# A new order of the loads, of K's first transform products and of the whole plan in a fused SSM convolution and gated MLP

## The chip, the cores and the metric

The kernel runs on one core of a Trainium2 chip. The time is that of the device in microseconds for one launch, and the median over several executions is compared. The core has five engines that work side by side: PE (matmul), DVE (vector), ACT (activations), POOL (GpSimd) and SP, which here only issues transfers. Each engine takes its instructions in order. SP, ACT and POOL can issue transfers between the memory outside the core (DRAM) and the one inside (SBUF); the products of PE go to PSUM and are evicted from there by DVE or ACT.

## What is computed

A layer norm, a long convolution whose filter K is generated from a state space model, and a gated MLP, both on the normalized tokens, added to the input. There are 2048 tokens of 512 channels, 128 modes for each channel, and 1792 hidden columns; all tensors are bf16.

```python
xn = _layernorm(x)
# A: K = sum over modes n of C * exp(dt*A*l) * dt*B, l = 0 .. 2047, real part
P = jnp.exp(logdA[:, :, None] * l[None, None, :])
K = jnp.einsum("dn,dnl,dn->dl", Cc, P, dB).real
...
Yf = Uf * Kf[None, :, :, :]          # FFTs of 4096 of u = xn and of K
y = irfft2(Yf)[..., :L] + u * Dskip
# B:
h = _sigmoid(xn @ w_gate) * (xn @ w_up)
return x + y + h @ w_down
```

## The kernel before, in words

**The MLP** (`glu`). The tokens are worked in eight groups of 256. For each group PE multiplies the transposed tokens xnT with the up and the gate weights (tile W, 14 column blocks of 128 in chunks of four, L827; one product task is eight matmuls of 128x256), ACT takes the sigmoid, DVE multiplies, and PE multiplies with the down weights wd (L832). Group 0 and group 1 have their tokens transposed on PE (the "turn", L496, copied out as xnT by L358 on ACT or L359 on DVE); later groups by transfers. For group 0 the up products come first, then the gate ones. The last product of the group adds the input by a matmul with the identity (L837).

**The filter** (`params`, `hlevels`, `glevels`, `kgen`, `expand`). The parameters (six arrays, loaded in halves as raw00 to raw51: array, then block) become powers H and G by repeated complex multiplication on DVE (L645 to L648), in two blocks b of 256 channels with two halves c each. `kgen` multiplies them on PE (L732) and gets K, which is written to DRAM (kt_scr) and read back by `expand` in 19 shifted pieces to the tile kf.

**The convolution** is a transform in two steps. `spectrum_x` and `spectrum_k` make the first step's products with a constant matrix s1p (L790 for the tokens, L810 for K, eight products for a block: four groups m of four kf columns, two halves j), evict them and write them to DRAM (z_scr, zk_scr). `freq` reads these back in another layout, eight units per block: px and pkf (L960) are the second step's products, XX is their pointwise product (L980 on DVE, or L981 on ACT and then DVE), pv (L969) goes back one step, and its eviction G is written to v_scr. `inverse` reads v_scr (as tiles H, G, kf) and makes the last step's products py (L1008), which DVE adds to the output (L1012). `store` writes the output.

**The plan.** Each piece of work is one of 919 tasks, numbered in the order in which the functions add them. A planner outside the kernel has chosen three tables by its own costs, sizes and dependencies; at run time only the tables count. `emit` goes through ORDER and calls the tasks one after the other, so ORDER sets the order on every engine and queue. OTHER lists the tasks that run on their alternative engine: evictions and norms change between ACT and DVE, transfers between the queues of SP and POOL. SIDE picks, for each PSUM buffer, one of four areas A to D. Semaphore waits come from the overlap of the tiles that tasks read and write, in program order. The arguments `after`, `mb`, `rank` and the helper `seq`, which adds an edge between two tasks, only tell the planner what it may not do or what a transfer costs.

**The loads** (`loads`). SP issues nearly all. x0 and x1 (128 KB each), x2 (256 KB), x4, x8, x12 (512 KB each) are tokens; w1 with its start column (0, 512, 1024 with 512 KB each; 1536 with 256 KB) are the up weights, w0 the gate weights; the raw pieces have 64 KB; wd0 (1 MB) and wd8 (768 KB) are the down weights. The order on SP before: x0, raw00, ldt, x2, x8, raw20, raw40, raw50, raw30, raw41, w1 0, x4, w1 512, w1 1024, w1 1536, w0 0, x12, w0 512, w0 1536, w0 1024, raw21, raw51, raw11, raw01, wd8, raw31, wd0.

Tasks that the prediction names: 767, 702, 780, 741 and 832 are issues of SP in the late stage (reads of zk_scr for units 0, 1 and 5 of the second block, and writes of v_scr for units 4 and 7 of the first); 804 and 830 write v_scr for units 2 and 4 of the second block; norms 2, 4, 6, 14, 15 are the layer norm of one row block of 128 tokens each.

Of the kernel before, what the change touches and what calls it, by code (L numbers as in the profile page):

```python
# [24 lines left out]
NT = 16  # L25
# [4 lines left out]
ND = 256  # L30
# [187 lines left out]
class _Kernel:  # L218
# [145 lines left out]
    def loads(self):  # L364
# [39 lines left out]
        n0 = len(self.ld)  # L404
# [3 lines left out]
        for q in range(2, 6):  # L408
            raw(q, 0, mb=0.09)
# [12 lines left out]
        self.seq([self.ld["x0"], self.ld["raw00"]] + list(self.ld.values())[n0:n0 + 2])  # L422
        for t in list(self.ld.values())[n0 + 2:]:
            self.seq([self.ld["x2"], t])
# [324 lines left out]
    def expand(self, b):  # L749

        kf, kt, rk = self.kf[:].rearrange("p (i d) -> p i d", d=ND), self.kt_scr[b], 82 + 70 * b
        rows = kt[:].rearrange("h g d -> (h g) d")
        kfb = self.own("kf")
# [4 lines left out]
        def rd(out, in_, n):  # L758
            self.kfl.append(self.dma(lambda: out, lambda: in_, 1.7 * n * ND * 2 / 1048576, self.dump, rk, 512, alt="POOL", more=0.12,
                                     **(dict(use=[kfb]) if self.kfl else dict(take=[kfb]))))  # L760

        for i in range(2):
            rd(kf[0:16, 8 * i:8 * i + 8, :], kt[0:8, i::2, :].rearrange("h g d -> g h d"), 128)
        for v, r0 in enumerate((256, 256, 512, 544, 544, 544, 576, 257)):
            rd(kf[16:32, v::8, :], rows[r0:r0 + 32].rearrange("(p i) d -> p i d", i=2), 32)
        for v, n, r0 in ((0, 3, 288), (3, 3, 608), (6, 2, 289)):
            for i in range(2):
                rd(kf[32:64, 8 * i + v:8 * i + v + n, :], rows[r0 + i:r0 + i + 63:2].unsqueeze(1).to_broadcast([32, n, ND]), 32 * n)
        for v, n, r0 in ((0, 5, 352), (5, 7, 353), (12, 4, 354)):
            rd(kf[64:128, v:v + n, :], rows[r0:r0 + 127:2].unsqueeze(1).to_broadcast([64, n, ND]), 64 * n)  # L770
# [4 lines left out]
        self.kfls[b], self.kfbs[b] = self.kfl + [self.kfd], kfb  # L775
# [22 lines left out]
    def spectrum_k(self, b):  # L798
# [4 lines left out]
        for m in range(NT // 4):  # L803
            for j in range(2):
# [7 lines left out]
                t = add("PE", 0.44, mm, self.kfls[b] + [self.ld["s1p"]], rk, take=[pz], use=[self.kfbs[b]])  # L812
# [293 lines left out]
```

## Time and profile before

| | us |
|---|---|
| three executions | 231.98, 232.03, 233.49 |
| median | 232.03 |
| profiled execution, its own time | 232.98 |
| its span, first to last instruction | 231.2 |

The mean granted clock of PE is 0.999. The profiled execution is 1.8 us longer than its span (launch and end around it), and it is 0.95 us above the median. In the rows below times are us from the start of the span. A timeline row shows the start, the time until the last of its instructions ended, engine, line, operation and tiles, how many instructions were joined (xN), and in brackets how long the engine had been idle before and what ended that.

### The profile page before, as it was taken

The numbers are of one execution on the slowest core, as the hardware profiler recorded it, in microseconds if no ns is written. First come the engines' busy times: TensorE is split into PE (matmuls) and PEld (weight loads), VectorE is DVE, ScalarE is ACT, GpSimd is POOL, SyncE is SP. The second block draws the span as 40 slices with busy tenths as digits, with TensorE's granted clock in tenths as the row PEclk, the third lists the DMA queues.
The fourth block names the chain that finished last, engine by engine and source line by source line (L and its number), as shares of the span: only waits on it lengthen the run. The fifth ranks groups of instructions, "written<-read, shape, count | busy, mean of one in ns | idle before, by whom it ended". The sixth has DMA issues, their size and how long they took to land.

```text
span 231.2 us, 5364 instructions
## 1 busy us (share of the span) xinstructions
PE 212.2 (92%) x2150; PEld 148.7 (64%) x2169; DVE 200.1 (87%) x301; ACT 173.6 (75%) x218; POOL 40.2 (17%) x66
## 2 busy tenths in 40 slices
PE   3679998999999999999999999999988968999993
PEld 0368886677578876687446888667744545676641
DVE  3799989999999999999998999857697899958492
ACT  3199999999999989997754895427796589893500
POOL 2110060000010000050404121146020514011300
PEclk9999999999999999999999999999999999999999
DMA  6999911112212425435759888469878899995866
GB/s 164 246 331 348 315 60 34 25 23 71 91 57 48 115 31 136 116 91 138 220 198 284 291 255 240 100 166 224 217 269 286 235 285 295 303 269 161 257 252 220
DMA packets 55643, 43.16 MB, mean 187 GB/s; under 512 B 20785, under 2 KB 48642, under 8 KB 55362
## 3 DMA queue, kind: packets, MB, share of 16 engines
q1 hardware_dynamic: 51890, 33.16, 50.0%
q0 software_dynamic: 3312, 9.45, 13.2%
q8 instruction: 17, 0.28, 0.5%
q10 hardware_dynamic: 416, 0.20, 0.3%
q14 instruction: 8, 0.07, 0.1%
HBM read 25.86 MB, written 15.37 MB: 178 GB/s over the span
## 4 chain that ended last, share of the span: by engine, by line
PE 50%; ACT 20%; DMA 13%; DVE 11%; issue 3%; SPq 1%; ACTq 0%; DVEq 0%
PE po L832 15%; PE pg L827 12%; PE pu L827 9%; PE pk L732 4%; DMA zk<-zk_scr 4%; DMA zk_scr<-G 3%; DMA H<-v_scr 3%; PE pzx L790 2%; ACT ub L884 2%; DVE tB L645 2%; DMA acc<-in_A_u_dram 2%; DVE G L646 2%; PE pkf L960 2%; PE py L1008 2%; DVE G L647 1%
## 5 line engine op out<-in xcount | busy, mean ns | idle before, releaser
L827 PEld LDWEIGHTS <-W 128*128 128x128 bf16 x896 | 86.8, 98 | 19.5 <-issue 3.9
L827 PE MATMUL pg<-xnT,W 128*128 128x256 bf16 x496 | 60.5, 273 | 0.9 <-ACT ub L884 0.2
L827 PE MATMUL pu<-xnT,W 128*128 128x256 bf16 x400 | 47.6, 273 | 1.5 <-DMA W<-in_B_w_up_dram 1.1
L832 PE MATMUL po<-wd,hT 128*128 128x512 bf16 x133 | 31.9, 379 | 1.1 <-ACT hTb L358 0.6
L980 DVE TENSOR_TENSOR XX<-pkf,x 128x1024 bf16<-128x1024 f32 x20 | 23.9, 1221 | 6.4 <-PE pkf L960 6.1
L832 PEld LDWEIGHTS <-hT 128*128 128x128 bf16 x140 | 13.5, 98 | 15.8 <-issue 1.2
L892 ACT ACTIVATE ub<-pu 128x1024 bf16<-128x1024 f32 x16 | 16.5, 1030 | 5.3 <-PE pu L827 5.2
L645 DVE TENSOR_TENSOR tB<-G,gm 128x256 bf16<-128x256 bf16 (+4 forms) x20 | 19.6, 980 | 0.9 <-ACT G L707 0.6
L646 DVE TENSOR_TENSOR G<-G,gm 128x256 bf16<-128x256 bf16 (+4 forms) x20 | 19.6, 979 | 0.1
L889 ACT ACTIVATE hT<-pg 128x1024 bf16<-128x1024 f32 (+1 forms) x16 | 14.9, 928 | 6.0 <-PE pg L827 6.0
L358 ACT ACTIVATE zs<-pzx 128x1024 bf16<-128x1024 f32 x16 | 16.3, 1038 | 1.9 <-PE pzx L790 1.3
L358 ACT ACTIVATE x<-px 128x1024 bf16<-128x1024 f32 x14 | 14.3, 1027 | 4.2 <-PE px L960 3.3
L981 ACT ACTIVATE XX<-pkf 128x1024 bf16<-128x1024 f32 x12 | 12.2, 1027 | 6.3 <-PE pkf L960 6.3
L960 PEld LDWEIGHTS <-w 64*64 64x64 bf16 x384 | 9.7, 105 | 10.3 <-issue 8.7
L457 DVE BATCH_NORM_STATS2 stats<-acc 128x6 f32<-128x512 bf16 x16 | 10.6, 681 | 5.2 <-DMA acc<-in_A_u_dram 5.2
L960 PE MATMUL pkf<-zk,w 64*64 64x256 bf16 x256 | 12.3, 276 | 3.0 <-DMA zk<-zk_scr 1.1
L350 POOL DMA_DIRECT2D kf<-kt_scr x14 | 8.0, 581 | 29.0 <-DMA kt_scr<-ks 29.0
L358 ACT ACTIVATE G<-pv 128x1024 bf16<-128x1024 f32 x12 | 12.4, 1041 | 0.5 <-PE pkf L960 0.5
L832 PE MATMUL po<-wd,hTb 128*128 128x512 bf16 x55 | 12.7, 379 | 0.0
L891 DVE TENSOR_TENSOR hT<-hT,ub 128x1024 bf16<-128x1024 bf16 (+1 forms) x15 | 9.4, 632 | 3.4 <-ACT ub L892 3.4
L647 DVE TENSOR_TENSOR G<-G,tB 128x128 bf16<-128x128 bf16 (+4 forms) x20 | 11.4, 571 | 0.5
L648 DVE TENSOR_TENSOR G<-G,tB 128x128 bf16<-128x128 bf16 (+4 forms) x20 | 11.3, 566 | 0.1
(144 smaller groups left out, 356.1 us busy)
## 6 DMA issues: line engine op xcount, KB each, us to landing
z_scr<-zs SPq DMA_DIRECT2D x12, 256.0 KB, 2.3
zk<-zk_scr SPq DMA_DIRECT2D x11, 256.0 KB, 5.1
v_scr<-G SPq DMA_DIRECT2D x11, 256.0 KB, 4.9
acc<-in_A_u_dram SPq DMA_DIRECT2D x3, 512.0 KB, 6.3
W<-in_B_w_up_dram SPq DMA_DIRECT2D x3, 512.0 KB, 7.2
W<-in_B_w_gate_dram SPq DMA_DIRECT2D x3, 512.0 KB, 8.4
zk_scr<-G SPq DMA_DIRECT2D x6, 256.0 KB, 2.7
out_dram<-acc SPq DMA_DIRECT2D x6, 256.0 KB, 2.3
```

The lines of the kernel that those rows point to most:

```text
L358: return self.p.add("ACT", 0.17 + n / 1190, lambda: nc.scalar.activation(out=dst(), in_=src(), func=ACT.Identity), after, rank, alt=("DVE" ...
L645: ops = [(2, lambda: tt(out=tv(), in0=l, in1=mb(1), op=ALU.mult), [], [tB], []), (2, lambda: tt(out=o, in0=l, in1=mb(0), op=ALU.mult), [], ...
L646: (2, lambda: tt(out=o, in0=l, in1=mb(0), op=ALU.mult), [], [], []),
L647: (1, lambda: tt(out=o[:, :, 0], in0=o[:, :, 0], in1=tv()[:, :, 1], op=ALU.add), [0, 1], [], [tB]),
L648: (1, lambda: tt(out=o[:, :, 1], in0=o[:, :, 1], in1=tv()[:, :, 0], op=ALU.subtract), [0, 1], [], [tB])]
L827: nc.tensor.matmul(p[:, lo + n, :], W[:, i, kt, k * 128:(k + 1) * 128], xT[:, kt, :], start=kt == 0, stop=kt == KT - 1)
L832: nc.tensor.matmul(po[:, jj, :], hT[:, k, jj * 128:(jj + 1) * 128], wd[:, k, :], start=k == 0, stop=k == FT - 1 and self.outs[i // GT].eng ...
L889: e1 = add("ACT", 0.17 + n * 256 / 1190, lambda hk=hk, n=n, pg=pg: nc.scalar.activation(out=hk(), in_=pg[:, 0:n, :], func=ACT.Sigmoid), mg ...
L892: e2 = add("ACT", 0.17 + n * 256 / 1190, lambda uk=uk, pk=pk: nc.scalar.activation(out=uk(), in_=pk(), func=ACT.Identity), mu + [e1], rk + ...
L960: nc.tensor.matmul(p[o:o + 64, par, h, :], self.w3[i:i + 64, w, 64 * g:64 * g + 64], z[i:i + 64, 2 * h + c, :], start=True, stop=True, til ...
L980: prod = lambda xo=xo, x1=x1, src=None: nc.vector.tensor_tensor(out=xo(), in0=src(), in1=x1[:, 0], op=ALU.mult)
L981: ek = add("ACT", 1.03, lambda xo=xo, flat=flat: nc.scalar.activation(out=xo(), in_=flat(), func=ACT.Identity), [mk, e] + ([] if o else se ...
```

## The change

It changes four things. The number of tasks and their numbering stay as they are.

1. The planner is told a larger size for the four transfers raw20 to raw50 (0.15 MB in place of 0.09).
2. Behind x0 and raw00 the next eight loads are fixed: ldt, x2, w1 0, raw20, raw30, raw40, raw50, w1 512; all others may come only behind w1 512. Before, only ldt and x2 were fixed.
3. In `expand` each read notes which groups m of K's first products use its columns, and a product in `spectrum_k` depends, for the planner, on the reads of its own group alone (and on the add of Dskip for group 0) in place of on all 19.
4. New tables ORDER, OTHER and SIDE.

```diff
         for q in range(2, 6):
-            raw(q, 0, mb=0.09)
+            raw(q, 0, mb=0.15)
...
-        self.seq([self.ld["x0"], self.ld["raw00"]] + list(self.ld.values())[n0:n0 + 2])
-        for t in list(self.ld.values())[n0 + 2:]:
-            self.seq([self.ld["x2"], t])
+        self.seq([self.ld["x0"], self.ld["raw00"]] + list(self.ld.values())[n0:n0 + 8])
+        for t in list(self.ld.values())[n0 + 8:]:
+            self.seq([self.ld["w1512"], t])
...
-        def rd(out, in_, n):
+        need = [[] for _ in range(NT // 4)]
+
+        def rd(out, in_, n, at):
...
+            for m in {i // 4 for i in at}:
+                need[m].append(self.kfl[-1])
...
-        self.kfls[b], self.kfbs[b] = self.kfl + [self.kfd], kfb
+        need[0].append(self.kfd)
+        self.kfls[b], self.kfbs[b] = need, kfb
...
-                t = add("PE", 0.44, mm, self.kfls[b] + [self.ld["s1p"]], rk, take=[pz], use=[self.kfbs[b]])
+                t = add("PE", 0.44, mm, self.kfls[b][m] + [self.ld["s1p"]], rk, take=[pz], use=[self.kfbs[b]])
...
 ORDER = (
-    0, 2, 1, 3, 33, 29, 4, 5, 20, 7, 36, 9, 10, 37, 8, 93, 352, 27, 38, 94, 6, 43, 39, 353, 13, 44, 11, 354, 12, 40,
...
+    0, 2, 33, 1, 4, 29, 3, 5, 6, 7, 36, 8, 9, 93, 37, 352, 10, 94, 11, 38, 353, 20, 44, 39, 13, 354, 12, 40, 355, 22,
...
 OTHER = (
...
```

The new tables, in words:

- SP's load order becomes x0, raw00, ldt, x2, w1 0, raw20, raw30, raw40, raw50, w1 512, x8, x4, w1 1024, x12, w1 1536, w0 0, raw41, w0 1536, raw51, raw31, w0 1024, w0 512, raw21, wd8, raw01, raw11, wd0.
- On PE the turn of group 1 comes between the first two up products of group 0 and the rest (before: behind the first two gate products), and four up products of group 1 come before the second chunk of group 0's gate products (before: three behind it).
- Norms 2, 4, 6 and 14 go from ACT to DVE, norm 15 and the copy of group 1's xnT from DVE to ACT, one eviction of K (b 0, c 1) from DVE to ACT, the third up eviction of group 3 from ACT to DVE. In the late stage some more evictions change engine.
- SP issues 136 transfers in place of 152, POOL 74 in place of 58.
- In the late stage four half-chunks of the last group's up and gate products stand earlier among the units of the second block, and the reads and writes of the scratch tensors stand in another order.

More of the change, by code (lines that the diff above doesn't have):

```diff
@@ L756, in expand @@
             self.kfls, self.kfbs = {}, {}
-        def rd(out, in_, n):
+        need = [[] for _ in range(NT // 4)]
+        def rd(out, in_, n, at):
             self.kfl.append(self.dma(lambda: out, lambda: in_, 1.7 * n * ND * 2 / 1048576, self.dump, rk, 512, alt="POOL", more=0.12,
                                      **(dict(use=[kfb]) if self.kfl else dict(take=[kfb]))))
+            for m in {i // 4 for i in at}:
+                need[m].append(self.kfl[-1])
         for i in range(2):
-            rd(kf[0:16, 8 * i:8 * i + 8, :], kt[0:8, i::2, :].rearrange("h g d -> g h d"), 128)
+            rd(kf[0:16, 8 * i:8 * i + 8, :], kt[0:8, i::2, :].rearrange("h g d -> g h d"), 128, range(8 * i, 8 * i + 8))
         for v, r0 in enumerate((256, 256, 512, 544, 544, 544, 576, 257)):
-            rd(kf[16:32, v::8, :], rows[r0:r0 + 32].rearrange("(p i) d -> p i d", i=2), 32)
+            rd(kf[16:32, v::8, :], rows[r0:r0 + 32].rearrange("(p i) d -> p i d", i=2), 32, (v, v + 8))
         for v, n, r0 in ((0, 3, 288), (3, 3, 608), (6, 2, 289)):
             for i in range(2):
-                rd(kf[32:64, 8 * i + v:8 * i + v + n, :], rows[r0 + i:r0 + i + 63:2].unsqueeze(1).to_broadcast([32, n, ND]), 32 * n)
+                rd(kf[32:64, 8 * i + v:8 * i + v + n, :], rows[r0 + i:r0 + i + 63:2].unsqueeze(1).to_broadcast([32, n, ND]), 32 * n,
+                   range(8 * i + v, 8 * i + v + n))
         for v, n, r0 in ((0, 5, 352), (5, 7, 353), (12, 4, 354)):
-            rd(kf[64:128, v:v + n, :], rows[r0:r0 + 127:2].unsqueeze(1).to_broadcast([64, n, ND]), 64 * n)
+            rd(kf[64:128, v:v + n, :], rows[r0:r0 + 127:2].unsqueeze(1).to_broadcast([64, n, ND]), 64 * n, range(v, v + n))
         dsk = self.small["dsk"]
@@ L1022 @@
 ORDER = (
[40 rows of a table removed]
-OTHER = (
[5 rows of a table removed]
-SIDE = ("03332012210033023211000201203232202110003022031213013123212030131230110102102301302001213213030032132203123103"
-        "22310210011310213102331321031321223303212320220222121020011310232231131203013130")
[40 rows of a table added]
+OTHER = (
[5 rows of a table added]
+SIDE = ("32320102103010312130020031013101233313312212322030012120130213330323012031231221032103103300031132102131332000"
+        "02132103212120233202123211231113232212313332200100010221312323201102332003222103")
 @with_exitstack
```

88 rows, old and new, of tables (ORDER, OTHER) are left out of this document.

## The prediction

> **What bounds the kernel now.** I read the page first (busy shares, then its chain that ended last), then the table of windows, and then the timelines of the stages in which PE, the matmul engine, is not full.
>
> ```profile
> PE 212.2 (92%) x2150; PEld 148.7 (64%) x2169; DVE 200.1 (87%) x301; ACT 173.6 (75%) x218; POOL 40.2 (17%) x66
> ...
> PE 50%; ACT 20%; DMA 13%; DVE 11%; issue 3%; SPq 1%; ACTq 0%; DVEq 0%
> ```
>
> The first line is meant as a budget: 212.2 us of matmuls in a span of 231.2, so at most 19 us can be won by any new order, and DVE has only 31 us of slack. The second says that the chain runs through PE for only half of its length. So the idle places count, and the windows say where they are (columns: stretch, then busy time of PE, PEld, DVE, ACT, POOL, the granted clock, the DMA share, GB/s):
>
> ```profile
> 0.00:10.00 10.00, 4.11 (x9) 1.29 (x10) 4.55 (x16) 1.88 (x2) 2.27 (x10) 1.00 0.74 202
> 10.00:20.00 10.00, 8.36 (x76) 7.12 (x76) 9.76 (x26) 9.30 (x22) 1.28 (x3) 1.00 1.01 327
> 20.00:30.00 10.00, 9.64 (x90) 8.43 (x90) 10.00 (x16) 9.97 (x12) 0.00 (x0) 1.00 1.08 312
> 30.00:40.00 10.00, 9.30 (x77) 7.33 (x76) 9.18 (x31) 10.00 (x13) 3.80 (x3) 1.00 0.07 17
> ...
> 120.00:130.00 10.00, 9.97 (x111) 6.82 (x110) 8.96 (x13) 6.28 (x9) 2.62 (x4) 1.00 0.86 267
> ...
> 170.00:180.00 10.00, 8.68 (x110) 4.30 (x111) 8.34 (x9) 7.01 (x8) 1.36 (x3) 1.00 0.86 278
> 180.00:190.00 10.00, 7.63 (x159) 4.46 (x149) 9.31 (x10) 7.79 (x8) 3.74 (x5) 1.00 0.88 257
> 190.00:200.00 10.00, 8.89 (x184) 6.26 (x184) 9.45 (x10) 9.34 (x11) 2.97 (x4) 1.00 0.98 295
> ```
>
> Three things are to be seen. From 10 to 30 us the DMA engines are full (share 1.01 and 1.08), and PE is short of 10 us by 1.64 and 0.36. In the middle PE is full, with 9.97 of 10 us. From 170 to 200 us PE loses 1.32 + 2.37 + 1.11 = 4.8 us again. The granted clock is 1.00 throughout, so no time comes from it.
>
> **The ramp: the load order (parts 1 and 2 of the diff).** The change takes x8 (512 KB) and x4 (512 KB) from in front of the second up-weight slice, and x12 goes in front of the fourth up slice and of the first gate slice. These are the PE rows of that stretch and the DMA issues behind it:
>
> ```profile
> 12.31 1.91 PE L827 MATMUL pu<-xnT,W 128*128 128x256 bf16 x16 [0.34 <-ACT xnT L358]
> 15.34 4.54 PE L827 MATMUL pu<-xnT,W 128*128 128x256 bf16 x40 [1.12 <-DMA W<-in_B_w_up_dram]
> 20.00 1.91 PE L827 MATMUL pg<-xnT,W 128*128 128x256 bf16 x16
> ```
> ```profile
> 21.75 0.61 PE L496 MATMUL pt<-ident,xn 128*128 128x128 bf16 x8
> ```
> ```profile
> 11.14 2.77 SPq L350 DMA_DIRECT2D acc<-in_A_u_dram  x1
> 13.95 3.07 SPq L350 DMA_DIRECT2D W<-in_B_w_gate_dram  x3
> ```
> ```profile
> acc<-in_A_u_dram SPq DMA_DIRECT2D x3, 512.0 KB, 6.3
> ```
> ```profile
> 22.52 1.91 PE L827 MATMUL pg<-xnT,W 128*128 128x256 bf16 x16 [0.17 <-ACT hT L358]
> ...
> 37.81 1.89 PE L832 MATMUL po<-wd,hT 128*128 128x512 bf16 x7 [0.58 <-ACT hTb L358]
> ...
> 47.78 0.59 PE L837 MATMUL po<-acc,ident 128*128 128x512 bf16 x2
> ```
>
> The anchor is the row at 47.78, which closes the first group of 256 tokens. The same PE tasks stand ahead of it in both orders, 33.2 us of them behind 12.31, so before lost 47.78 - 12.31 - 33.2 = 2.25 us there: 1.12 on the up weights, 0.58 on ACT's hTb, and 0.55 in small gaps.
>
> The first up product (12.31) waits for ACT's copy of the first transposed group, and that hangs on x0, x1, x2 and DVE, whose loads aren't moved: I cost it at nothing. DVE now builds the diagonal (L549) with one statistic less in front of it, yet the copy (L358) has more of the short activations of L576 ahead of it on ACT, and these eat that.
>
> The 1.12 us goes whole: at 327 GB/s a 512 KB transfer takes 1.6 us, two of them and a 64 KB piece leave, so the slice that arrived at 15.34 arrives near 12. What is late next is the fourth up slice and then the first gate slice. Before, x12 left SP at 11.14 + 2.77 = 13.91 and landed about 6.3 later, at 20.2. All that stood in front of x12 except one 64 KB piece, and x12 itself, now stand in front of the end of the first gate slice (and nothing else does), so that lands near 20.2 as well. PE will want it at 12.31 + 1.91 + 4.54 + 0.6 (the turn of the second group, the row at 21.75; it is moved forward between the first up products, and its two norms are now both on DVE, done by about 14) = 19.35. So PE waits some 0.95 us in all for these two slices, and I leave 0.25 of the small ACT gaps. The 0.58 goes, because ACT has less to do in the ramp: four norms go from it to DVE, one norm and one copy come back (their prices are in the next part), a net 0.80 x 3 - 1.03 = 1.4 us. After: 1.2 us lost against 2.25, a gain of 1.05. Bounds: nothing at all if the gate slice lands 1 us later (the share above 1 says that this stream is at its limit), 2.0 if both slices come in time.
>
> **DVE's bill for it.** DVE pays 0.41 for each norm moved to it, and gets back other pieces:
>
> ```profile
> 9.25 0.41 DVE L486 TENSOR_SCALAR xn<-acc,m_f,rinv 128x512 bf16<-128x512 bf16 x1
> ...
> 19.86 0.80 ACT L490 ACTIVATE xn<-acc,nb,rinv 128x512 bf16<-128x512 bf16 x1
> ...
> 23.37 0.68 DVE L359 COPY xnT<-pt 128x1024 bf16<-128x1024 bf16 x1
> ```
> ```profile
> 11.23 1.03 ACT L358 ACTIVATE xnT<-pt 128x1024 bf16<-128x1024 bf16 x1
> ```
> ```profile
> 123.90 1.22 DVE L648 TENSOR_TENSOR G<-G,tB 128x2048 bf16<-128x2048 bf16 x1
> 125.03 1.22 DVE L913 TENSOR_TENSOR acc<-po,acc 128x1024 bf16<-128x1024 f32 x1
> 127.16 1.21 DVE L359 CAST ks<-pk 128x1008 bf16<-128x1008 f32 x1 [0.91 <-PE pk L732]
> ```
> ```profile
> 124.94 2.78 PE L732 MATMUL pk<-H,G 128*128 128x84 bf16 x64
> ```
>
> Up to the second block's powers DVE has three norms more net (1.23), one product with the up-projection more (the third ub of group 3, 128x1024 from f32: 1.22 like L913's), and less a copy of 0.68 and a K eviction of 1.21: +0.56 us. DVE's rows at 123.90 and 125.03 show no idle time before them, and PE's K products start at 124.94, just as L648 ends (123.90 + 1.22, less the overlap of two operations). So PE's gain of 1.05 meets a DVE that is 0.4 to 0.6 later, PE's products of the other groups cover part of it, and I keep 0.6 of the 1.05 behind 145 us. Bounds: -0.4 to 1.05.
>
> **K's products and their loads (part 3).** The change of `need` alters only what the planner believes. In both kernels the hardware waits for the overlapping pieces of kf that were written ahead in program order, so at run time part 3 is worth nothing by itself; it works through the order. Late stage, before:
>
> ```profile
> 170.52 4.99 DMA zk_scr<-G
> ...
> 175.60 1.24 DVE G L359
> ...
> 176.86 2.73 DMA zk_scr<-G
> ...
> 181.31 8.61 DMA zk<-zk_scr
> ...
> 208.69 1.24 DVE G L359
> ...
> 209.94 2.85 DMA v_scr<-G
> ...
> 213.54 5.82 DMA H<-v_scr
> ```
> ```profile
> zk<-zk_scr SPq DMA_DIRECT2D x11, 256.0 KB, 5.1
> ```
> ```profile
> 207.01 0.76 POOL L350 DMA_DIRECT2D v_scr<-G  x1 [10.05 <-ACT G L358]
> ```
> ```profile
> 185.97 0.41 PE L960 MATMUL pkf<-zk,w 64*64 64x256 bf16 x8 [0.50 <-DVE acc L913]
> ...
> 187.77 0.87 PE L960 MATMUL pkf<-zk,w 64*64 64x256 bf16 x16 [0.55 <-ACT x L358]
> ...
> 189.97 0.63 PE L960 MATMUL pkf<-zk,w 64*64 64x256 bf16 x16 [1.11 <-DMA zk<-zk_scr]
> ```
>
> In this chain the last eviction of K's spectrum waits for a buffer (4.99 us of a DMA), is done at 176.84, is written until 179.59, and only then can the second block's reads start, the slowest of them 8.61 us. In the new order the eight products stand about as late on PE (they end near 174, an estimate: before, the eviction that had to wait for its buffer, at 175.60, was of the last of them), but a buffer of that ring is free by then, so the last write lands near 174 + 1.24 + 2.73 = 178, or 177 if it is evicted by ACT: 1.6 to 2.6 us sooner. Against that, the first read of the second block (task 767) is now on SP behind a buffer that comes free only near 180, with four more issues (702, 780, 741, 832) behind it on SP. Net 16 issues move from SP to POOL. POOL idles between its issues (10.05 us before the row at 207.01), so I cost them at nothing; where that cover goes, one issue is 0.76 us. At the median of 5.1 that read lands at 185.1, and PE wants it at about 185 (an estimate from PE's order: its row at 185.97 belongs to the next unit), so some 0.5 us of wait stays there. Of the 2.16 us of the three waits above I take 1.0 as won, also because four half-groups of the last group's products now stand between these reads. Bounds: 0 and 2.2 won, 3 lost.
>
> **The tail** from the last pv (208.0) to the end has the same PE work and the same chain (208.69: eviction 1.24, write 2.85, read 5.82) in both orders: nothing.
>
> **The sum.** 0.6 + 1.0 = 1.6 us: span 231.2 to 229.6. The profiled execution took 232.98 by its own time, 1.8 over its span, and 0.95 over the median of the three runs, 232.03. So: that execution 231.4, the median 230.4.
>
> [...] Of the v writes in the last stage three more come from POOL than before, where the row at 207.01 is the one. [...]
>
> **The rivals.**
> 1. The late stall goes entirely (the ring slot was its cause): all 2.16 us of the three waits and 1 us more of the 4.8 that PE loses from 170 to 200, 3.2 in place of 1.0: 230.4 - 2.2 = 228.2; for it speaks the chain, which runs through zk_scr from 170.5 to 190. Against it speaks task 767.
> 2. The change does nothing: the gate slices are 1 us later because the DMA share is 1.01 to 1.08, DVE's +0.56 eats the rest, and the late reads are as late: 232.0.
> 3. The other side: SP, which issues in order, stands behind 767 with four issues. If its read, out at 180, takes the 8.61 us of the slowest one instead of the median, it lands at 188.6, and PE, which wants it near 185 and has its other late products queued behind it, waits 3.5 us in that one place, with the old waits as they are: 232.0 - 0.6 + 3.5 = 234.9. From 0.6 us of added wait on the kernel is slower than before, from 2.9 us on by over 1%. For it speaks the slow read in the chain, against it the median.
> [...]
>
> **How the numbers follow.** Chances: forecast 0.40 (its own range 229.0 to 231.8), late stall gone 0.16, nothing 0.18, SP blocked 0.20, POOL writes 0.06. The predicted time is the forecast's, 230.4. A measurement of this kernel tells about 1% from no change, so faster is below 229.7, slower above 234.35. Faster: rival 1 whole and 0.14 of the forecast's 0.40: 0.30. Slower: 0.17 of the third rival, and 0.05 from rivals 2 and 4 with something more going wrong: 0.22. The rest, 0.48, is the same. The range leaves out what is under 227.4 (rival 1 with the whole ramp gain) and above 235.0.
>
> **What would show it.** Right: no wait at the second up slice, one of 0.3 to 1 us at the first gate slice; the row at L837 near 46.7; K's products of the second block at 124.5 to 125.5; the last zk_scr write landing near 177 to 178; the last pv near 206.4. Wrong: the first up product later than 12.6 (a moved DVE or ACT piece in front of it), K's products later than 126 (DVE is the bound), or a wait of over 1.5 us for DMA zk behind 180 (SP is blocked).

## The result and the profile after

| | before | after |
|---|---|---|
| median, 22 executions each, one chip (us) | 232.22 | 231.28 |
| lowest to highest (us) | 230.78 to 235.49 | 229.16 to 232.97 |
| ratio of the times, 95% interval | | 0.995 (0.993 to 0.998) |
| profiled execution: time, span, mean clock | 232.98, 231.2, 0.999 | 232.66, 230.9, 0.998 |

The changed kernel is faster by 0.9 us, half a per cent: inside the 1% that the prediction called no change, and well short of the 1.6 us that its sum gave. The profiled execution of after lies 1.4 us above its own median, that of before 0.8, so the two spans differ by only 0.3 us. The ratio leaves out executions over 1.5% above the fastest of their kernel (three of after, the profiled one among them, and one of before); the medians of all give 0.996. Times within a trace are compared below; the totals are compared by the medians.

In after.py the lines behind L755 stand six further down: the products of L827, L832 and L837 are L833, L838 and L843, the last product's L1008 is L1014.

First the budget of after's page, then its table of windows (columns as before):

```profile
PE 213.6 (92%) x2169; PEld 147.2 (64%) x2169; DVE 201.1 (87%) x304; ACT 172.4 (75%) x215; POOL 50.6 (22%) x82
...
PE 63%; DMA 15%; ACT 13%; DVE 3%; issue 3%; SPq 2%; POOL 0%; ACTq 0%; DVEq 0%
```
```profile
0.00:10.00 10.00, 6.12 (x29) 3.03 (x30) 5.83 (x22) 3.23 (x7) 2.94 (x11) 1.00 0.77 221
10.00:20.00 10.00, 7.21 (x66) 5.73 (x65) 9.56 (x21) 9.91 (x20) 0.62 (x2) 1.00 1.03 331
20.00:30.00 10.00, 10.00 (x91) 8.76 (x92) 9.90 (x23) 9.94 (x11) 1.25 (x1) 1.00 0.95 298
30.00:40.00 10.00, 10.00 (x89) 8.62 (x88) 9.60 (x26) 10.00 (x15) 2.80 (x5) 1.00 0.11 24
...
170.00:180.00 10.00, 9.40 (x103) 4.68 (x105) 7.55 (x9) 6.77 (x8) 0.63 (x1) 1.00 0.95 313
180.00:190.00 10.00, 9.26 (x186) 6.21 (x182) 9.28 (x11) 9.30 (x12) 5.26 (x7) 1.00 0.99 290
190.00:200.00 10.00, 8.35 (x163) 5.84 (x164) 9.91 (x11) 8.21 (x10) 2.71 (x4) 1.00 0.83 247
...
210.00:220.00 10.00, 7.95 (x48) 4.42 (x46) 5.73 (x6) 1.08 (x2) 2.59 (x4) 1.00 0.71 214
```

For comparison before's last stretch of this kind:

```profile
210.00:220.00 10.00, 9.61 (x69) 6.56 (x68) 6.61 (x8) 4.55 (x6) 2.15 (x3) 1.00 0.69 208
```

PE's share of the chain rises from 50% to 63%, and from 20 to 40 us PE is now full. It does 2.0 us more in the first 10 us and 1.15 less in the next, 1.6 us more from 180 to 190, and 1.7 us less from 210 to 220: something was won early and late, and was given back at the end.

To see where, I follow a **lead**: how much earlier PE starts a given task than in before, less the PE work that stands ahead of it in one of the two orders only. The rows of PE on which it rests:

```profile
10.83 1.91 PE L833 MATMUL pu<-xnT,W 128*128 128x256 bf16 x16 [0.76 <-ACT xnT L358]
16.08 1.92 PE L833 MATMUL pu<-xnT,W 128*128 128x256 bf16 x16 [1.15 <-ACT wp L596]
18.46 1.05 PE L833 MATMUL pu<-xnT,W 128*128 128x256 bf16 x8 [0.46 <-DMA W<-in_B_w_up_dram]
19.93 1.92 PE L833 MATMUL pg<-xnT,W 128*128 128x256 bf16 x16 [0.42 <-DMA W<-in_B_w_gate_dram]
45.78 0.59 PE L843 MATMUL po<-acc,ident 128*128 128x512 bf16 x2
123.75 2.58 PE L732 MATMUL pk<-H,G 128*128 128x84 bf16 x64
```

The close of the first group (45.78) has the same PE work ahead of it in both orders, so its lead is 47.78 - 45.78 = 2.0 us. Around 141 us it is 2.3, at the last pv 3.5 (208.00 against some 204.5), at the last products py 0.5. A second trace of the same kernel (the first experiment) gives 1.95, 2.0, 2.6 and 0.4. So in these two the change won 2 us in the ramp, kept them through the middle, added 0.6 to 1.2 us in the late stage, and lost 2.2 to 3.0 us between the last pv and the last py. Kernels of the experiments below that differ from after only behind some point say how far this repeats up to there: in eight traces with the changed ramp the close of the first group lies at 45.75 to 46.44, so 1.3 to 2.0 us are won there, and in the seven of them that have the changed late stage as well it adds 0.6 to 2.1.

The tail, first in before: the last pv, the first of the last reads of v_scr on SP, and PE's only longer wait.

```profile
208.00 0.63 PE L969 MATMUL pv<-XX,w 64*64 64x256 bf16 x16
...
219.50 1.02 PE L1008 MATMUL py<-H,s2p 128*128 128x512 bf16 x4 [0.34 <-DMA H<-v_scr]
```
```profile
212.96 1.18 SPq L350 DMA_DIRECT2D H<-v_scr  x2
```

The tail of after: PE's rows, then ACT's and SP's, then the chain (start, us, what).

```profile
204.01 1.07 PE L975 MATMUL pv<-XX,w 64*64 64x256 bf16 x32
...
216.94 1.04 PE L1014 MATMUL py<-H,s2p 128*128 128x512 bf16 x4 [1.32 <-DMA H<-v_scr]
...
221.19 1.89 PE L1014 MATMUL py<-G,s2p 128*128 128x512 bf16 x8 [1.92 <-DMA G<-v_scr]
```
```profile
204.70 2.12 ACT L358 ACTIVATE G<-pv 128x1024 bf16<-128x1024 f32 x2 [0.46 <-PE pv L975]
```
```profile
200.60 6.61 SPq L350 DMA_DIRECT2D v_scr<-G  x2
207.30 0.53 SPq L350 DMA_DIRECT2D kf<-v_scr  x1
210.75 1.18 SPq L350 DMA_DIRECT2D H<-v_scr  x2
```
```profile
212.03 9.02 DMA G<-v_scr
221.05 0.14 issue
221.19 2.75 PE py L1014 x12
...
```

The last two pv now run back to back on PE (32 products in the row at 204.01), and ACT evicts both, one behind the other. The last eviction ends at 206.82, yet the reads of v leave SP only at 210.75. PE then waits 1.32 and 1.92 us for them, against 0.34 in before.

### The profile page after: what moved, and what is told of

It is laid out like the page before. It is cut to its first block, busy times and chain, and to the rows that moved or that the text cites. A ratio compares the mean times of both kernels' runs of the same rounds, so it can differ in the third digit from the quotient of the medians.

```text
span 230.9 us, 5382 instructions
## 1 busy us (share of the span) xinstructions
PE 213.6 (92%) x2169; PEld 147.2 (64%) x2169; DVE 201.1 (87%) x304; ACT 172.4 (75%) x215; POOL 50.6 (22%) x82
## 4 chain that ended last, share of the span: by engine, by line
PE 63%; DMA 15%; ACT 13%; DVE 3%; issue 3%; SPq 2%; POOL 0%; ACTq 0%; DVEq 0%
PE po L838 16%; PE pg L833 15%; PE pu L833 14%; DMA W<-in_B_w_gate_dram 4%; PE pk L732 4%; DMA G<-v_scr 4%; PE py L1014 3%; PE pzx L796 3%; PE pv L975 2%; DMA W<-in_B_w_up_dram 2%; DMA H<-z_scr 2%; DMA hTb<-z_scr 2%; ACT ub L890 2%; PE pzk L816 2%; ACT xn L490 2%
## 5 line engine op out<-in xcount | busy, mean ns | idle before, releaser
L833 PEld LDWEIGHTS <-W 128*128 128x128 bf16 x896 | 86.0, 98 | 21.9 <-issue 4.4
L833 PE MATMUL pg<-xnT,W 128*128 128x256 bf16 x496 | 60.2, 273 | 0.5 <-DMA W<-in_B_w_gate_dram 0.4
L833 PE MATMUL pu<-xnT,W 128*128 128x256 bf16 x400 | 49.1, 273 | 2.4 <-ACT wp L596 1.1
L838 PE MATMUL po<-wd,hT 128*128 128x512 bf16 x140 | 32.5, 379 | 0.0
L838 PEld LDWEIGHTS <-hT 128*128 128x128 bf16 x140 | 13.5, 98 | 15.2 <-issue 0.2
L986 DVE TENSOR_TENSOR XX<-pkf,x 128x1024 bf16<-128x1024 f32 x16 | 19.3, 1220 | 4.2 <-PE pkf L966 4.1
L987 ACT ACTIVATE XX<-pkf 128x1024 bf16<-128x1024 f32 x16 | 16.1, 1031 | 7.3 <-PE pkf L966 7.3
L898 ACT ACTIVATE ub<-pu 128x1024 bf16<-128x1024 f32 x14 | 14.5, 1034 | 2.2 <-PE pu L833 2.2
L350 POOL DMA_DIRECT2D kf<-kt_scr x18 | 10.2, 575 | 21.5 <-PE pu L833 21.4
L350 POOL DMA_DIRECT2D z_scr<-zs x6 | 3.4, 569 | 51.4 <-ACT zs L358 51.4
L1018 DVE TENSOR_TENSOR acc<-py,acc 128x1024 bf16<-128x1024 f32 x8 | 9.5, 1219 | 4.9 <-PE py L1014 4.9
L358 ACT ACTIVATE x<-px 128x1024 bf16<-128x1024 f32 x11 | 11.1, 1029 | 3.4 <-PE px L966 3.4
L838 PE MATMUL po<-wd,hTb 128*128 128x512 bf16 x56 | 12.7, 379 | 0.0
L986 DVE TENSOR_TENSOR XX<-XX,x 128x1024 bf16<-128x1024 bf16 x16 | 10.6, 683 | 1.5 <-ACT XX L987 1.5
L358 ACT ACTIVATE G<-pv 128x1024 bf16<-128x1024 f32 x11 | 11.3, 1036 | 0.7 <-PE pv L975 0.7
```

Source lines behind the costliest of these rows:

```text
L350: go = lambda e: lambda: q[e].dma_start(out=out(), in_=in_(), **(dict(transpose=True) if transpose else {}))
L358: return self.p.add("ACT", 0.17 + n / 1190, lambda: nc.scalar.activation(out=dst(), in_=src(), func=ACT.Identity), after, rank, alt=("DVE" ...
L833: nc.tensor.matmul(p[:, lo + n, :], W[:, i, kt, k * 128:(k + 1) * 128], xT[:, kt, :], start=kt == 0, stop=kt == KT - 1)
L838: nc.tensor.matmul(po[:, jj, :], hT[:, k, jj * 128:(jj + 1) * 128], wd[:, k, :], start=k == 0, stop=k == FT - 1 and self.outs[i // GT].eng ...
L898: e2 = add("ACT", 0.17 + n * 256 / 1190, lambda uk=uk, pk=pk: nc.scalar.activation(out=uk(), in_=pk(), func=ACT.Identity), mu + [e1], rk + ...
L986: prod = lambda xo=xo, x1=x1, src=None: nc.vector.tensor_tensor(out=xo(), in0=src(), in1=x1[:, 0], op=ALU.mult)
```

## The experiments

Each comparison is with the kernel before on the same chip; the interval is 95%.

### The change once more

The changed kernel without an edit, to see how well trace and time repeat.

> The changed kernel once more, unedited, for a second profile: in the first one PE was 3.4 us ahead of the kernel before at the last pv and only 0.5 us ahead at the end, with waits of 1.3 and 1.9 us for the last reads of v_scr. Theory 'the tail is a chain of transfers': the same waits stand here, 2 to 3.5 us together, and the time is 0.3 to 0.8% under before. Rival 'that one execution was slow': the waits come to under 1 us, PE's lead of 3 us reaches the end, span near 228.

Measured: 231.94 us against 232.86, ratio 0.993 (0.989 to 0.997). The gain of about 0.5% stands. The tail of this trace, its chain:

```profile
200.09 8.81 DMA v_scr<-G
...
209.01 1.03 ACT G L358
...
210.06 2.36 DMA v_scr<-G
```

Here the last eviction waits 2.39 us for its buffer, which an earlier write of v (issued at 200.09, landed at 208.90) still reads. The two executions lose the lead in the same place, by different members of one chain: eviction, write, read.

### x8 back in front

One piece of part 2 undone: x8 (task 20) leaves SP right behind x2 again.

```diff
-    0, 2, 33, 1, 4, 29, 3, 5, 6, 7, 36, 8, 9, 93, 37, 352, 10, 94, 11, 38, 353, 20, 44,
+    0, 2, 33, 1, 4, 29, 3, 5, 20, 6, 7, 36, 8, 9, 93, 37, 352, 10, 94, 11, 38, 353, 44,
```

> The changed kernel with one load moved: x8 (512 KB) again directly behind x2 on SP, everything else as changed. Theory 'x8 behind x2 slows x2': x2 lands near 7.4 in place of 5.8 and the first up product starts at 12.0 to 12.4 in place of 10.8. Rival 'DVE's order, with one statistic less ahead of the diagonal, did it': x2 lands near 5.8 and the first up product stays at 10.8 to 11.2. For the end: if the gate weights set the ramp, the first gate product stays near 19.9 and the time is within 0.3 us of the changed kernel; if the start itself counts, it is 1 to 1.5 us longer.

Measured: 233.40, ratio 1.004 (1.000 to 1.007). PE's rows, with two 2 us stretches (the clock is the third number from the end):

```profile
11.39 1.04 PE L560 MATMUL pc<-kf 128*128 128x128 bf16 x4 [2.33 <-DMA kf<-in_A_B_re_dram]
...
14.39 1.91 PE L833 MATMUL pu<-xnT,W 128*128 128x256 bf16 x16 [0.26 <-ACT xnT L358]
```
```profile
10.00:12.00 2.00, 0.61 (x4) 0.56 (x5) 1.83 (x8) 0.31 (x2) 1.18 (x2) 0.74 1.04 308
12.00:14.00 2.00, 2.00 (x14) 1.86 (x13) 1.97 (x6) 0.69 (x1) 0.00 (x0) 0.50 0.91 321
```

The 512 KB stand in front of raw20, which lands at 11.3 us; PE waits 2.33 us for it, and its granted clock is 0.50 from 12 to 14 us. The first up product is 3.6 us later than in after, and the lead at the close of the first group is -1.1. One transfer in the wrong place costs the whole gain. The 64 KB piece raw20, which is not moved itself, lands 3 us later than in after (8.3). x2 landed at 6.6, against 5.8 in after and 7.4 in before; over all traces its landing lies at 5.3 to 7.4 with x8 behind it and at 5.5 to 6.7 without, so that x8 delays x2 is not shown.

### The loads alone, and the plan alone

The first puts the new first ten loads, and behind them x8, x4, w1 1024, w1 1536 and the rest, into before's order (two statistics of x8's rows stand further behind on DVE, so that DVE doesn't wait for x8 early). The second keeps the new plan with all loads in before's order (four statistics moved).

```diff
-    0, 2, 1, 3, 33, 29, 4, 5, 20, 7, 36, 9, 10, 37, 8, 93, 352, 27, ...
+    0, 1, 4, 5, 6, 7, 8, 9, 10, 11, 20, 13, 12, 14, 15, 22, 27, ...
```

> The kernel before with its loads alone changed: the first ten in the new fixed order, then x8, x4, and the rest in the old order (raw41 behind x12); two statistics of x8's rows stand three tasks later on DVE, so that DVE doesn't wait for x8. All else is the old plan. Theory 'x8 slows x2': x2 lands near 5.9, the first up product starts near 11, the wait of 1.1 us at the second up slice goes, and the end of the first group (L837) is at 46.3 to 46.9 in place of 47.8; the old tail has little wait for its reads, so 0.5 to 1 us of it is kept at the end: 231.2 to 231.7 against 232.2. Rival 'the gain of the ramp comes from the new plan (order and engines), not from the loads': L837 stays at 47.3 or later and the time is that of before within 0.3 us.

```diff
-    0, 2, 33, 1, 4, 29, 3, 5, 6, 7, 36, 8, 9, 93, 37, 352, 10, 94, 11, ...
+    0, 1, 4, 5, 20, 7, 9, 10, 8, 27, 6, 13, 11, 12, 14, 15, 22, 16, ...
```

> The new plan with the whole load order of the kernel before (x8 directly behind x2, w1 512 behind x8 and x4, x12 behind the first gate slice); four statistics of DVE stand later so that DVE doesn't wait for x12. The counterpart of the run with the new loads in the old plan. Theory 'the plan's late stage makes the gain, the loads almost nothing, since the tail takes what is beyond about 0.5 us': PE is 1 us later at the end of the first group (L843 at 46.8 to 47.6 in place of 45.8 to 46.4), still 2 us ahead of before at the last pv, and the time is within 0.4 us of the changed kernel. Rival 'the new loads make the gain': the time is that of before within 0.3 us, or longer.

Measured: loads alone 232.65, ratio 1.001 (0.997 to 1.004); plan alone 232.39, ratio 0.997 (0.993 to 1.000). Both together are the change, 0.995 and 0.993. PE of the loads alone:

```profile
11.17 3.65 PE L827 MATMUL pu<-xnT,W 128*128 128x256 bf16 x32 [0.34 <-ACT xnT L358]
15.98 2.79 PE L827 MATMUL pu<-xnT,W 128*128 128x256 bf16 x24 [1.15 <-DMA W<-in_B_w_up_dram]
...
46.82 0.59 PE L837 MATMUL po<-acc,ident 128*128 128x512 bf16 x2
```

PE of the plan alone, and its clock in stretches of 2 us:

```profile
16.34 6.21 PE L833 MATMUL pu<-xnT,W 128*128 128x256 bf16 x40 [2.59 <-DMA W<-in_B_w_up_dram]
```
```profile
14.00:16.00 2.00, 0.00 (x0) 0.00 (x0) 2.00 (x5) 2.00 (x6) 0.00 (x0) 1.00 1.11 357
16.00:18.00 2.00, 1.66 (x14) 1.40 (x15) 1.82 (x4) 2.00 (x6) 0.00 (x0) 0.89 1.13 343
18.00:20.00 2.00, 2.00 (x11) 1.40 (x10) 1.01 (x1) 2.00 (x5) 0.00 (x0) 0.50 1.04 374
20.00:22.00 2.00, 2.00 (x16) 1.57 (x15) 1.79 (x4) 0.65 (x2) 0.00 (x0) 0.76 1.13 329
```

The loads alone win 1.0 us at the close of the first group, in the trace they keep it to the end (1.4; this execution is 1.1 us under its median), and in the median nothing of it is to be seen. The plan alone is 0.3 us behind there, for its order of PE wants the second up slice early and gets it at 16.34, and it is 1.2 ahead at the last pv and 0.1 behind at the end. So the ramp's 2 us need both, and the late gain belongs to the plan. The medians order the four kernels, but loads alone and plan alone have overlapping intervals, and so have the plan alone and the change itself.

### Half of each plan

The new plan's first 510 tasks in front of the old plan's rest, and the reverse (OTHER and SIDE with them), to carry a lead, or a lag, into each late stage.

```diff
-    521, 677, 258, 623, 622, 533, 522, 690, 266, 624, 523, 261, 532, 524, ...
+    521, 677, 258, 623, 622, 533, 522, 690, 266, 624, 523, 625, 626, 627, ...
```

> The first 510 tasks of the new plan (to about 125 us: loads, ramp, first K products), then all other tasks in the order, on the engines and in the PSUM areas of the old plan. PE reaches the cut some 2 us ahead of the kernel before. Theory 'the new order of the late stage and of the tail gives the lead away': the old late stage carries the 2 us through (as it carried 1.1 to 1.4 us in the profile of the run with the new loads alone), span near 229 and 0.6 to 0.9% under before. Rival 'the end is set by the transfers, whoever orders them': under 0.8 us of the 2 are left at the end, the time within 0.3% of before.

```diff
-    0, 2, 33, 1, 4, 29, 3, 5, 6, 7, 36, 8, 9, 93, 37, 352, 10, 94, 11, ...
+    0, 2, 1, 3, 33, 29, 4, 5, 20, 7, 36, 9, 10, 37, 8, 93, 352, 27, 38, ...
```

> The mirror image: the first 510 tasks of the old plan with the old load order, then the rest of the new plan. PE comes to the late stage without a lead and gains there what the new order of the zk writes and reads gives, 1.5 to 2 us at unit 0 of the second block. Theory 'the tail gives the lead away': the waits before the last py products (3.2 us in the changed kernel) become smaller by the 2 us that are missing at its start, and the time is that of the changed kernel within 0.5 us, though the ramp is the old one. Rival 'each stage adds its own gain': it is 1.5 to 2 us longer than the changed kernel, so 0.4 to 0.7% over before.

Measured: 235.87, ratio 1.013 (1.007 to 1.018), and 235.34, ratio 1.015 (1.011 to 1.020). As totals both say nothing, because the seam costs. In the first, PE waits there:

```profile
138.46 3.54 PE L833 MATMUL pg<-xnT,W 128*128 128x256 bf16 x16 [2.67 <-ACT ub L898]
```

As traces they say something: the first comes out of its seam with a lag of 3.3 us, and has 3.4 at the last pv and 2.9 at the last py, so the old late stage passes on what it gets. The second goes from a lag of 1.1 at the seam to a lead of 0.3 at the last pv and -0.2 at the last py.

### More bytes in the tail

Two reads of 256 KB each from v_scr into a buffer that nothing uses any more, on ACT's queue behind the last write of v, in after and in before. They add work that the reference does not need.

```diff
+            if n == 599:
+                self.extra()
+    def extra(self):
+        to = self.gm[:].rearrange("p l r d -> p (l r d)")
+        fr = self.v_scr[1][:].rearrange("s (j i) d -> s j (i d)", j=2)
+        for n in range(2):
+            self.nc.scalar.dma_start(out=to[:, 1024 * n:1024 * n + 1024].rearrange("p (j d) -> p j d", j=2),
+                                     in_=fr[:, :, 512 * n:512 * n + 512])
```

> The changed kernel with two more reads of 256 KB from v_scr into a tile that nothing uses any more, issued by ACT as soon as the last v write has landed; nothing waits for them. Theory 'the tail is a chain of transfers at their full rate': the eight last reads share with them, their last one lands 1.5 to 2 us later (512 KB at 270 to 350 GB/s) and the end moves by 1 to 2 us. Rival 'order of PE and the engines': it moves by under 0.4 us.

> The same two reads in the kernel before. Its PE waits only 0.3 us for the last reads in the profile, so if its tail is bound by PE, some of the delay is hidden there: 0.3 to 1 us longer. If its tail hangs on the transfers as that of the changed kernel does: 1 to 2 us.

Measured: after with them 233.37, ratio to before 1.007 (1.004 to 1.009), so 2.1 us over after's 231.28; before with them 234.58, ratio 1.012 (1.008 to 1.016), so 2.4 us over 232.22. By the ratios it is 1.007 - 0.995 = 1.1% (unrounded) and 1.2%, 2.6 and 2.7 us. The waits of PE, first in after with the reads, then in before with them (line numbers three up):

```profile
PE py L1017 <- DMA H<-v_scr: 2.7, 1, 2.7
...
PE py L1017 <- DMA G<-v_scr: 1.9, 2, 1.8
```
```profile
PE py L1011 <- DMA G<-v_scr: 1.8, 1, 1.8
```

At the 208 and 214 GB/s of the two rows for 210 to 220 us above, 512 KB are 2.5 us (an estimate). Both tails pay about that in full, so both end by transfers, the old one too, although its PE looks busy. The new one was not made sensitive by the change; it had the same transfers still to do.

### Down products in front of the waiting py

The order at PE's end: the last two down products (605 and 606; 609 is the add behind them), or one (605), stand in front of the py that wait, and one entry of SIDE, a PSUM area, changes with them. The third run keeps the order and puts the last eviction of pv (task 855) on DVE; the fourth has both edits.

```diff
-    879, 603, 604, 891, 893, 608, 894, 901, 610, 910, 903, ... 915, 605, 899, 918, 916, 606, 912, 913, 609, 917)
+    879, 603, 604, 605, 891, 893, 608, 894, 606, 610, 609, 910, 901, ... 915, 918, 916, 917, 899, 912, 913)
```

> The changed kernel with its last 27 tasks in another order: the two last down products (L838, 3.0 us together) stand ahead of the py products that wait for the last reads of v_scr, not behind them; the adds and stores follow, one py takes another PSUM area. Theory 'the tail is a chain of transfers and PE's work behind it': the down products fill the two waits, the last read lands where it did (221), and behind it stand only py products, one add and a store: 228.0 to 229.3, that is 2 to 3 us less than the changed kernel. Rival 'the stores or the adds on DVE set the end': under 0.7 us less.

```diff
+    879, 603, 604, 605, 891, 893, 608, 894, 610, 910, 901, 903, ... 915, 606, 899, 918, 916, 912, 913, 609, 917)
```

> The changed kernel with only one of the two last down products (1.7 us) ahead of the py products that wait for the last reads, the other behind them as it was, and PSUM areas chosen so that no py waits for an add of the down products (in the run with both moved, one did, 0.8 us). Theory 'the end is last read plus adds and stores': PE fills a wait and is done 1.3 to 1.7 us earlier, but the last stores hang on the py adds, so the end moves by 0 to 0.5 us. Rival 'PE's work behind the reads sets the end': 1.3 to 1.7 us earlier.

```diff
 OTHER = (
-    826, 830, 831, 839, 843, 844, 845, 852, 858, ...
+    826, 830, 831, 839, 843, 844, 845, 852, 855, 858, ...
```

> The changed kernel with one eviction on the other engine: that of the last pv (unit 6 of the second block) on DVE, as in the kernel before, in place of ACT, where it stands behind another eviction. Theory 'the end hangs on the last v write and the reads behind it': the write leaves SP 0.4 to 1 us earlier, the last read lands that much earlier, and the time is 0.3 to 1 us under the changed kernel. Rival 'the transfers of this stage are at their limit, whenever the last write leaves': the last read lands at 222 to 222.6 as before, under 0.3 us.

Both of the last two edits:

> Both edits together: the last v eviction on DVE and one down product ahead of the waiting py products. If each helps by itself they should add: 0.5 to 1.5 us under the changed kernel, 229.8 to 230.8 against 231.3. Rival: the transfers set the end and both are within 0.4 us of the changed kernel.

Measured, in this order: 234.11, ratio 1.006 (1.003 to 1.009); 233.13, ratio 0.999 (0.996 to 1.002); 231.07, ratio 0.991 (0.988 to 0.995); 232.21, ratio 0.996 (0.993 to 1.000). Filling the waits doesn't pay: with both down products in front, PE is done with its last product 2.2 us ahead of before, but the py then wait for a PSUM area, and the transfers do not end sooner: DVE's last add ends at 227.01 (227.69 in after), and the span ends 5.4 us behind it (3.2 in after), with the last stores in between. PE of that kernel, the window at the end of the one with one product in front, and DVE's eviction in the third:

```profile
222.46 1.89 PE L1014 MATMUL py<-G,s2p 128*128 128x512 bf16 x8 [0.78 <-DVE acc L927]
```
```profile
220.00:229.00 9.00, 2.48 (x12) 0.92 (x10) 3.58 (x4) 0.00 (x0) 1.08 (x2) 0.83 0.64 234
```
```profile
205.96 1.22 DVE L359 CAST G<-pv 128x1024 bf16<-128x1024 f32 x1
```

In the window PE has 2.5 us of work in 9: the end only waits for what is stored. This trace is the fastest of its twelve executions (230.93). The eviction on DVE stood behind a DVE product and ended at 207.18, no sooner than ACT's at 206.82 in after, so in this trace its mechanism was not put to the test; but the execution profiled (233.76) lies 2.7 us above the median, and what the others did is not known. Its median is the lowest of all twelve, but its interval overlaps the unedited kernel's 0.993 (0.989 to 0.997), and I don't count it as a better kernel.

## Why the prediction was right, and where it was not

The forecast was 230.4, a change too small to be told; 231.28 was measured, within 1% and within the range. That it came so near is in part luck: at the last pv PE was 2.6 to 3.5 us ahead where the prediction had 1.6 (206.4), and the tail, which it left at nothing, took most of that back. Of the sum's two terms the ramp's was too small and the late stage's about right; a third, set at zero, was not zero.

**The ramp, 1.05 won: 2.0 measured (1.3 to 2.0 over eight traces).** The prediction held the first up product at 12.31 and costed it at nothing. It starts at 10.83, 11.30 in the second trace. DVE shows what stood in front of it, after first, then before:

```profile
5.88 0.69 DVE L457 BATCH_NORM_STATS2 stats<-acc 128x6 f32<-128x512 bf16 x1
...
7.42 0.42 DVE L549 TENSOR_TENSOR kf<-ident,g 128x512 bf16<-128x512 bf16 x1
```
```profile
7.39 0.69 DVE L457 BATCH_NORM_STATS2 stats<-acc 128x6 f32<-128x512 bf16 x1 [1.33 <-DMA acc<-in_A_u_dram]
...
9.58 0.42 DVE L549 TENSOR_TENSOR kf<-ident,g 128x512 bf16<-128x512 bf16 x1
```

In before DVE waited 1.33 us for x2 in front of the diagonal. x2's issue isn't moved, but it landed 1.6 us sooner, and the diagonal stands 2.2 us earlier. The prediction took "x2 isn't moved" for "x2 lands as before". Why it lands sooner stays open, and part of it is scatter: three traces with before's loads and early plan (before, the one with two more reads, and the old plan's half with the new late one) have x2 at 7.4, 6.8 and 5.3, and their first up product at 12.31, 12.74 and 11.38; eight with the changed ramp have it at 10.83 to 11.86. Its other ramp numbers held: the first gate product starts at 19.93 (19.35 + 0.95 = 20.3 predicted), behind waits of 0.46 and 0.42 for the two slices it named. The wait at the second up slice did not go: 1.15 us, but on a PSUM area that ACT holds (0.35, for the slice, in the second trace).

**DVE's bill, 1.05 clipped to 0.6: not paid.** K's products of the second block start at 123.75 (124.03 in the second trace), ahead of the predicted 124.5 to 125.5. DVE's whole line comes earlier, its L648 of 123.90 in before at 121.33, so its 0.56 us of added work was covered, and the lead of 2 us came through the middle whole.

**The late stage, 1.0 won: 0.6 to 1.2 measured (0.6 to 2.1 over seven traces), and the mechanism held.** SP's rows with the last write of K's spectrum and with the read that the third rival feared:

```profile
172.02 2.07 SPq L350 DMA_DIRECT2D zk_scr<-G  x3
...
177.04 0.36 SPq L350 DMA_DIRECT2D zk<-zk_scr  x1
177.45 0.54 SPq L350 DMA_DIRECT2D v_scr<-G  x1
```
The last of the three writes in the first row lands at 176.9 (177 to 178 predicted, 179.59 before). Task 767 leaves at 177.04, not near 180, and the next issue follows at 177.45, so SP isn't blocked, and PE's list of waits has no row for zk (one of 0.4 us in the second trace): rival 3 falls. Of rival 1 the stall did go, and PE's 4.8 us lost from 170 to 200 became 0.60 + 0.74 + 1.65 = 3.0. Part 3 shows in the order alone, as predicted: three of K's transform products of the first block now stand ahead of one of K's reads, and three of the second block ahead of the add of Dskip. What that is worth by itself no run tells.

**The tail, "nothing": 2.2 to 3.0 lost. This is the step that failed.** The prediction found the same PE work and the same chain in both orders and gave the tail no term. But PE's 3.5 us of lead do not reach the transfers behind it. Measured from the last pv's start, the first of the last eight reads leaves after 5.0 us in before and 6.3 and 7.1 in the two traces of after. Over all kernels of this study it is 4.4 to 5.2 with the old late plan, and 5.9 to 7.1 with the new. The reads then take about 10 us in either order (9.4 to 10.9 without added reads). So of 3.5 us at the last pv, 2.2 are left at the first read (212.96 to 210.75), 1.05 at the last landing (222.7 to 221.65), and 0.3 at the end. Two members of the chain are seen to be longer. From the pv's start to the issue of the last write it is 1.9 us with the old late plan and 2.2 to 3.0 with the new (in most of these two evictions in a row on ACT, where before had one each on ACT and DVE), and 4.7 in the second trace of after, where a ring buffer was held by a write that took 8.8 us. From that issue to the first read it is 2.5 to 3.3 us in the four traces with the old late plan and 2.4 to 4.7 in the ten with the new, 3.4 or more in seven of them. In the first trace of after, of 1.3 us more, 0.4 are the eviction's and 0.9 the write's. Why the write lands later, whether by the other writes and the reads of the first block in flight with it, no run isolates: the one edit aimed at the eviction did not move it. What is shown is that the end hangs on transfers: 512 KB more cost 2.1 to 2.7 us in both kernels, and down products in front of the py, which fill PE's waits, bring nothing.

**POOL's writes (chance 0.06): no sign.** No run shows that a write issued from POOL delays the end. In the first trace of after the last two (tasks 830 and 804) left at 204.53 and 206.01 and landed 4.76 and 3.93 us later, at 209.29 and 209.94; SP's last one left at 206.84 and landed 3.82 us later, at 210.66.

**The rival that the change does nothing** is excluded for the total (the interval ends at 0.998), but it describes one half: the loads alone give 1.001.

So the sum read 0.6 + 1.0 + 0 = 1.6, and came out as about 2.0 + 1.1 - 2.8 = 0.3 in the spans of the two traces, 0.9 in the medians. Some of the rest may lie in the clock. On the chip of the first experiments 20 of 35 executions of before had a mean clock under 0.9955 and a median of 232.94, the other 15 one of 232.63; of 12 of after there, and of 22 in the result, none had. So some 0.2 of the 0.9 us there may be the clock's (an estimate: 232.86 - 232.63). The loads alone had 8 of 12, at 233.48, and four at 232.20, which may hide a small gain of theirs. On the two other chips 27 of 35 and 11 of 17 executions of before were of this kind, the first 0.9 us longer than the rest, the second 0.8 shorter, so the size stays open. No profile of before caught one, so where in the kernel it happens, and why the change avoids it, stays open too.

## What to carry to other kernels

A lead on the compute engine is worth what the last chain of transfers lets through (here 3.5 us at the last pv became 0.3 at the end): before summing gains, take the last dependent transfers (eviction, write, read) and ask what starts them in the new order, because "the same operations" is not "the same chain" when its evictions stand behind one another and its writes land later. A load that isn't moved can land at another time when one in front of it is: with x8 in front (DMA share 0.90 from 5 to 10 us, 1.04 from 10 to 12) raw20 came 3 us later, at 11.3 in place of 8.3. A new load order and a new order of compute belong together: here each alone won little or nothing by the medians (1.001 and 0.997), and one 512 KB load in the wrong place cost the whole gain (1.004).

## What the runs showed of the hardware

Waits of PE of 1.95 to 2.67 us came with a lower granted clock, which cost up to 1.7 us more (an estimate from the clock of the stretches). In the plan alone PE is idle for 2.59 us until 16.34; then the granted clock is 0.89, 0.50 and 0.76 in the next three stretches of 2 us, so (0.11 + 0.50 + 0.24) x 2 = 1.7 us of full clock are missing. The kernel with x8 in front (wait 2.33; 0.74, 0.50 and 0.91 from 10 to 16 us), the two halves (2.67; 0.63 and 0.52 from 138 to 142; and 1.95; 0.60 and 0.54 from 16 to 20) and the tail of the kernel with the eviction on DVE (2.50; 0.91 and 0.92 in the two stretches of 10 us from 210) give 1.7 us each by the same sum. The single wait does not decide it: the first of the halves has another such stretch between 190 and 200 us (0.83), where its longest wait was 1.1; and the 1.15 us in the ramp of after, the 1.98 that end at 10.05 in before, and the 2.70 in the tail of after with two more reads left the clock at 1.00. What decides between these and those the traces don't show.
